# The values' products in 64x64 tiles of TensorE instead of 64x32, with another order of the operations

## The chip, the core and the metric

The kernel runs on one core of a Trainium2 chip. The metric is device time in microseconds (us) of one execution. Times of single instructions come from the trace of one profiled execution.

The engines are named as in the profile: PE is TensorE's matmul, PEld its weight load, DVE is VectorE, ACT is ScalarE, POOL is GpSimd, SP is SyncE, which here does nothing but issue DMAs. PSUM is the memory that PE writes.

## What is computed

Sliding-window attention with four sink positions, and behind it a gated layer whose gate is a causal convolution over five positions. Batch 4, 8 heads, 768 positions, 64 numbers per head, all in float32:

```python
scores = q @ k.transpose(0, 1, 3, 2) / sqrt(64)
keep   = (key < 4) | ((0 <= row - key) & (row - key < 128))
a      = softmax(where(keep, scores, -1e9))
x      = (a @ v), heads side by side -> (4, 768, 512)
gate   = sigmoid(sum over k of conv_w[k] * x shifted by 4 - k positions)
out    = (gate * (x @ w_val)) @ w_out
```

`w_val`, `w_out` and `conv_w` come as float64 and are decoded on the chip into a high and a low float32 part.

## The kernel before

The work is cut into 24 **steps**. Step s is one of 4 batches, one of 3 stretches of 256 positions (p = 0, 1, 2) and one of 2 groups of four heads; steps 2m and 2m+1 make **pair** m, for which the gated layer is computed. p is 0 for eight steps (0, 1, 6, 7, 12, 13, 18, 19) and over 0 for sixteen.

What a step does, with the names that the order uses:

- `kq`, `vv`: load k and q, or v, by SP (L236, L238, L245); three buffers each.
- `s0`, `s1` (`scores`, L391): 16 products each of 64x32 tiles of PE into one of two PSUM pairs `pr`; then DVE masks them (L396) and finds the maximum (L400 or L405).
- `e0`, `e1` (`exps`, L416) on ACT, `rec` the reciprocal of the sums, `norm` (L431) on POOL.
- `tx` (`probs_t`, L449): eight transposes on PE into a `pr` pair; `px` (DVE, L477 and L479) and `py` (ACT, L486) copy them to `wt`. `sk` transposes the sinks (L454).
- `vl` (`values`, L506): probabilities times v into the PSUM tile `xv`, of which there is one. For each of six blocks of keys (four where p = 0) there are four products (two heads by two groups), each cut in two halves of 32 output rows: 48 products a step, 32 where p = 0. Blocks have 64, 128, 192, 192, 128 and 64 moving columns (192, 192, 128, 64 where p = 0). Each float32 product runs as two loads and two matmuls, so that the trace has 96 (or 64) of each.
- `si` (`sinks`, L514) adds the sinks' share. `xc`, `xh`, `hd` (ACT, L521, L529, L533) copy x out, `c4` (POOL, L542) and `c0`, `c1` (DVE, L550) do the convolution out of `xv`. The values of step s+1 can start only when the convolution of step s has read `xv`.

For a pair, `v0` to `v3` (L569) multiply x by w_val, `g`, `h`, `l` gate (L588, L594, L598), `o0` to `o3` (L609) multiply by w_out and `t0`, `t1` (L613, L616) copy and store. `fill.n` is n matmuls on zeros. `scalars` (L100) reads the two numbers n_sink and window by two DMAs, each of which spreads 8 bytes to every partition; `flag` uses them at the very end.

Nothing is scheduled by the compiler: `ORDER` is a list of such names, written out, and each name's instructions go to the queues of their engines in that order. A load that stands behind another in the list stands behind it in SP's queue.

The inner lines of `values`:

```python
for e in range(2):
    r0 = o * D + e * QB                      # QB = 32, D = 64
    nc.tensor.matmul(acc[r0:r0 + QB, g, ...], v[js, g, n, e * QB:(e + 1) * QB],
                     t[js, g, n, a0:a1 + 1]...)
```

Of the kernel before, what the change touches and what calls it, by code (L numbers as in the profile page):

```python
# [36 lines left out]
wvl.0 masks fill.5 load_conv signs leads kq.0 conv_weights wva.0 blanks wvb.0 wvc.0 wvd.0 wvl.1 wva.1 s0.0
e0.0 s1.0 wvl.2 wva.2 fill.7 e1.0 wve.0 wvb.1 wvc.1 wvb.2 rec.0 kq.1 wvf.0 wvc.2 wvd.1 wol.0 woa.0 s1.1 e1.1
norm.0 s0.1 kq.2 e0.1 vv.0 fill.10 s1.2 e1.2 wve.1 wob.0 woc.0 tx.0 px.0 rec.1 fill.6 vv.1 py.0 sk.0 ts.0 sv.0
wvl.3 wod.0 wva.3 s0.2 e0.2 vl.0 kq.3 s0.3 wvf.1 si.0 xc.0 xh.0 norm.1 woe.0 c4.0 wvb.3 vv.2 wvd.2 wvc.3 tx.1  # L40
fill.6 px.1 wve.2 hd.0 rec.2 norm.2 wof.0 wvd.3 wve.3 e0.3 wol.1 kq.9 c0.0 c1.0 kq.4 tx.2 woa.1 wob.1 wvf.2
py.1 wol.3 sv.1 xl.0 sk.1 py.2 ts.1 wod.1 px.2 woc.1 vl.1 s1.3 si.1 wvf.3 sk.2 xc.1 ts.2 hd.1 c4.1 s0.4 xh.1
c0.1 e1.3 fill.4 rec.3 c1.1 e0.4 woe.1 woa.3 wob.3 xl.1 th.0 v0.0 v1.0 y0.0 g0.0 wol.2 woa.2 wod.3 wob.2
norm.3 s1.4 h0.0 th.1 l0.0 vl.2 si.2 xc.2 e1.4 v2.0 v3.0 woe.3 y1.0 woe.2 g1.0 tx.3 px.3 kq.6 s0.6 wof.1 o2.0
wod.2 wof.2 hd.2 c4.2 h1.0 xh.2 vv.4 py.3 rec.4 vv.3 l1.0 o0.0 c0.2 kq.5 s0.5 c1.2 e0.6 s1.6 wof.3 o1.0 t0.0
o3.0 e0.5 sk.3 ts.3 vv.6 th.2 norm.4 t1.0 vl.3 si.3 xh.3 xc.3 hd.3 sk.4 ts.4 xl.2 s1.5 xl.3 e1.5 c4.3 tx.4
v0.1 v1.1 px.4 rec.5 c0.3 vv.5 e1.6 c1.3 rec.6 v2.1 v3.1 kq.7 py.4 y0.1 g0.1 h0.1 s0.7 th.3 vl.4 norm.5 y1.1
g1.1 h1.1 s1.7 l0.1 kq.8 s1.8 l1.1 si.4 xc.4 c4.4 xh.4 o2.1 vv.8 o3.1 sv.6 hd.4 c0.4 tx.5 px.5 e0.7 e1.8 c1.4
o0.1 o1.1 t1.1 xl.4 e1.7 py.5 norm.6 tx.6 py.6 px.6 sk.5 ts.5 kq.15 rec.7 t0.1 vl.5 si.5 xc.5 c4.5 hd.5 xh.5
xl.5 vv.7 sk.6 ts.6 s0.9 norm.7 e0.9 s0.8 e0.8 c0.5 th.4 c1.5 rec.8 norm.8 v0.2 v1.2 tx.7 kq.10 py.7 v2.2 px.7  # L50
th.5 g0.2 s1.9 s1.10 h0.2 e1.9 vl.6 l0.2 si.6 xc.6 c4.6 hd.6 xh.6 sk.7 v3.2 ts.7 g1.2 h1.2 rec.9 l1.2 o2.2
e1.10 o0.2 o3.2 c0.6 c1.6 xl.6 sv.7 kq.11 tx.8 px.8 norm.9 s0.10 t1.2 py.8 vl.7 si.7 xc.7 hd.7 sk.8 ts.8 tx.9
kq.12 c4.7 xh.7 px.9 py.9 c0.7 xl.7 c1.7 e0.10 rec.10 o1.2 t0.2 v0.3 v1.3 th.6 s0.12 g0.3 th.7 s0.11 vv.10
e0.12 vl.8 s1.11 vv.13 si.8 h0.3 xc.8 c4.8 hd.8 xh.8 sk.9 ts.9 l0.3 e0.11 c0.8 v2.3 c1.8 norm.10 e1.11 v3.3
kq.13 g1.3 h1.3 o2.3 vv.9 s1.12 rec.11 s1.13 l1.3 vl.9 e1.12 vv.11 si.9 xc.9 hd.9 c4.9 tx.10 py.10 xh.9 o3.3
o0.3 o1.3 norm.11 px.10 rec.12 sv.13 tx.11 t1.3 c0.9 c1.9 sk.10 ts.10 s0.13 t0.3 py.11 px.11 kq.18 xl.9 th.8
vl.10 si.10 xl.8 v0.4 v1.4 xc.10 kq.14 c4.10 hd.10 xh.10 c0.10 c1.10 e1.13 e0.13 norm.12 v2.4 rec.13 g0.4
tx.12 s0.18 vl.11 sk.11 h0.4 v3.4 ts.11 si.11 py.12 px.12 norm.13 th.9 g1.4 h1.4 s1.14 s0.14 vv.12 xc.11 l0.4
l1.4 c4.11 hd.11 xh.11 sk.12 e0.14 ts.12 o0.4 o1.4 xl.11 c0.11 e1.14 c1.11 rec.14 o2.4 o3.4 sv.12 s0.15 xl.10
t0.4 vl.12 si.12 kq.16 xc.12 hd.12 xh.12 c4.12 tx.13 px.13 vv.22 t1.4 c0.12 th.11 c1.12 v2.5 e0.15 v3.5 g1.5  # L60
th.10 v0.5 v1.5 h1.5 g0.5 py.13 h0.5 sk.13 ts.13 norm.14 s1.15 e1.15 s1.18 vl.13 si.13 rec.15 kq.20 kq.17
e1.18 l0.5 l1.5 o0.5 s0.16 tx.14 px.14 o2.5 o3.5 xc.13 c4.13 vv.14 o1.5 hd.13 xh.13 e0.16 t1.5 norm.15 tx.15
c0.13 c1.13 sk.14 ts.14 th.12 py.14 px.15 vv.15 t0.5 s1.16 e0.18 xl.13 vl.14 si.14 xl.12 xc.14 c4.14 py.15
hd.14 xh.14 sk.15 th.13 ts.15 kq.19 v0.6 c0.14 c1.14 e1.16 v1.6 g0.6 rec.16 v2.6 vv.16 s0.17 rec.18 e0.17
s0.19 xl.14 vl.15 v3.6 g1.6 si.15 s1.19 vv.17 s1.17 norm.16 sk.16 ts.16 h0.6 l0.6 o0.6 h1.6 warm_up xc.15
hd.15 th.14 xh.15 e1.17 l1.6 c4.15 tx.16 o1.6 px.16 c0.15 c1.15 e0.19 rec.17 xl.15 v0.7 v1.7 g0.7 s0.20 py.16
# [5 lines left out]
rec.21 sk.19 ts.19 s1.22 s0.22 vl.19 h1.8 si.19 l1.8 sk.20 ts.20 h0.8 xc.19 l0.8 o0.8 kq.23 o1.8 c4.19 hd.19
xh.19 norm.21 vv.20 e1.22 o2.8 c0.19 c1.19 e0.22 rec.22 tx.21 py.21 xl.19 t0.8 px.21 s1.23 vl.20 s0.23 e1.23
si.20 norm.22 xc.20 c4.20 v0.9 v1.9 o3.8 th.18 hd.20 g0.9 xh.20 xl.20 e0.23 t1.8 tx.22 c0.20 v2.9 v3.9 rec.23
py.22 c1.20 h0.9 sk.21 norm.23 px.22 ts.21 th.19 g1.9 vl.21 si.21 tx.23 px.23 l0.9 o0.9 xc.21 h1.9 c4.21 l1.9
hd.21 xh.21 c0.21 o2.9 o3.9 t1.9 o1.9 c1.21 sk.22 vl.22 t0.9 ts.22 si.22 xc.22 py.23 xh.22 sk.23 xl.21 v0.10
# [773 lines left out]
```

## Time and profile before

| | us |
|---|---|
| time, median of 3 runs | 273.45 (273.35 to 273.96) |
| the profiled execution's own time | 275.11 |
| its span, first to last instruction | 273.3 |
| mean granted TensorE clock | 0.992 of 2.4 GHz |
| PE busy | 258.1 (94%) |
| DVE, ACT, POOL busy | 205.5, 188.3, 175.6 |

The profiled execution took 275.11 us, of which 273.3 are the span. Busy shares say how long an engine had something in work; several small matmuls lie over one another on PE, so that its busy time is no measure of how full the array is. What an operation costs on PE is read from the start of its first matmul to the start of the operation behind it.

### The profile page before, as it was taken

To read this page: it belongs to the slowest core of one execution; us is meant where nothing else is said; L and a number is where in the kernel's file an instruction comes from. 1 tells how busy PE (TensorE), PEld (TensorE's weight loads), DVE (VectorE), ACT (ScalarE), POOL (GpSimd) and SP (SyncE) were. 2 spreads that over 40 slices of the span, in tenths; PEclk is the share of its full clock that TensorE was granted. 3 is DMA by queue.
4 is the path that set the end of the run, shared out by engine and by line. 5 is a ranking of instruction groups with operands and counts; after the bars stand their busy time and mean duration, and the time that the engine had idled before them with its cause. 6 is when DMAs were issued, how large, how long until landed. Compare 5 with 4: busy or idle time off the path is not lost.

```text
span 273.3 us, 11512 instructions
## 1 busy us (share of the span) xinstructions
PE 258.1 (94%) x4779; PEld 218.1 (80%) x4784; DVE 205.5 (75%) x561; ACT 188.3 (69%) x667; POOL 175.6 (64%) x233
## 2 busy tenths in 40 slices
PE   7889999999999999999999999899799999999990
PEld 2456569789888899889889888799689899898970
DVE  5886999968879788978878788688577878724530
ACT  2899999788887859856567875687467667353410
POOL 6187886776758781797855575784883867734330
PEclk9999999999999999999999999999999999999996
DMA  6998355047274346448025764204336311040202
GB/s 202 389 377 294 135 155 166 2 142 256 60 208 133 104 140 177 141 135 260 4 55 185 240 180 138 60 4 133 126 93 228 115 41 42 4 137 2 77 5 82
DMA packets 27402, 37.07 MB, mean 136 GB/s; under 512 B 2256, under 2 KB 23760, under 8 KB 27344
## 3 DMA queue, kind: packets, MB, share of 16 engines
q1 hardware_dynamic: 26528, 35.48, 40.4%
q8 instruction: 39, 0.64, 1.0%
q10 hardware_dynamic: 816, 0.79, 0.9%
q14 instruction: 19, 0.16, 0.2%
HBM read 29.97 MB, written 6.29 MB: 133 GB/s over the span
## 4 chain that ended last, share of the span: by engine, by line
PE 82%; ACT 8%; DVE 3%; DMA 2%; issue 2%; POOL 1%; ACTq 0%
PE ac L609 25%; PE ac L569 24%; PE xv L506 11%; PE pr L391 10%; PE pr L449 7%; PE xv L514 3%; ACT w L416 3%; DMA raw<-in_w_val_dram 2%; DVE sg L550 1%; PE ac L454 1%; ACT wv_p L137 1%; ACT wv_p L156 1%; POOL xl L537 0%; DVE wt L477 0%; ACT xt L521 0%
## 5 line engine op out<-in xcount | busy, mean ns | idle before, releaser
L550 DVE SCALAR_TENSOR_TENSOR sg<-xv,cw,sg 128x256 f32<-128x256 f32 x192 | 77.4, 473 | 10.1 <-POOL sg L542 8.7
L431 POOL TENSOR_TENSOR wx<-w,sm 128x512 f32<-128x512 f32 x48 | 49.1, 1046 | 7.7 <-DVE sm L423 7.6
L416 ACT ACTIVATE w<-pr,ngm 128x132 f32<-128x132 f32 x136 | 48.5, 369 | 1.8
L569 PE MATMUL ac<-xh,wvh 128*128 128x256 f32 x192 | 48.3, 286 | 0.0
L598 POOL TENSOR_TENSOR gl<-sg,gh 128x512 fp32r<-128x512 f32 x24 | 31.0, 1295 | 26.8 <-ACT gh L594 26.7
L569 PE MATMUL ac<-xh,wvl 128*128 128x256 f32 x192 | 47.2, 280 | 0.0
L542 POOL TENSOR_TENSOR sg<-xt,cw 128x512 f32<-128x512 f32 x24 | 25.0, 1043 | 28.4 <-ACT xt L521 26.0
L391 PE MATMUL pr<-k,q 64*32 64x168 f32 x1536 | 36.5, 307 | 4.1 <-DVE ngm L400 1.4
L609 PE MATMUL ac<-woh,gh 128*128 128x512 f32 x96 | 39.2, 408 | 0.0
L506 PE MATMUL xv<-wt,v 64*32 64x192 f32 (+2 forms) x2048 | 37.0, 275 | 1.8 <-issue 1.3
L506 PEld LDWEIGHTS xv<-wt,v 64*32 64x32 f32 x2048 | 34.8, 105 | 4.2 <-issue 2.3
L609 PE MATMUL ac<-wol,gh 128*128 128x512 f32 x96 | 38.0, 395 | 0.0
L609 PE MATMUL ac<-woh,gl 128*128 128x512 f32 x96 | 37.9, 395 | 0.0
L569 PEld LDWEIGHTS ac<-xh,wvh 128*128 128x128 f32 x192 | 36.1, 188 | 0.5 <-issue 0.3
L569 PEld LDWEIGHTS ac<-xh,wvl 128*128 128x128 f32 x192 | 36.2, 189 | 0.2
L391 PEld LDWEIGHTS pr<-k,q 64*32 64x32 f32 x1536 | 24.1, 106 | 11.9 <-ACT w L416 3.2
L537 POOL TENSOR_TENSOR xl<-xt,xh 128x512 fp32r<-128x512 f32 x24 | 30.9, 1289 | 3.6 <-ACT xt L521 1.7
L569 PE MATMUL ac<-xl,wvh 128*128 128x256 f32 x192 | 30.6, 280 | 0.3 <-POOL xl L537 0.3
L594 ACT ACTIVATE gh<-sg 128x512 fp32r<-128x512 f32 x24 | 15.2, 632 | 19.9 <-DVE sg L588 19.8
L396 DVE COPY_PREDICATED pr<-low,pr 128x256 f32<-128x256 uint8 x48 | 20.3, 422 | 9.9 <-PE pr L391 8.8
L416 ACT ACTIVATION_READ_ACCUMULATOR w<-pr,ngm 128x1 f32 x136 | 27.6, 203 | 0.0
L521 ACT ACTIVATE xt<-xv 128x512 f32<-128x512 f32 x24 | 14.4, 598 | 18.9 <-PE xv L514 18.7
...
## 6 DMA issues: line engine op xcount, KB each, us to landing
...
out_dram<-osb SPq DMA_DIRECT2D x24, 256.0 KB, 2.2
q<-in_qt_dram SPq DMA_DIRECT2D x23, 256.0 KB, 5.0
...
v<-in_vt_dram SPq DMA_DIRECT2D x8, 256.0 KB, 3.8
...
```

What stands on the lines that cost most here:

```text
L391: nc.tensor.matmul(ss[e * QB:(e + 1) * QB, j, c * n + x0:c * n + x1], q[js, g, (4 * c + e) * QB:(4 * c + e + 1) * QB], k[js, g, (2 * c + e ...
L396: nc.vector.copy_predicated(sv[:, :, :, :D], low[:, None, None, :].to_broadcast([P, 2, 2, D]), sv[:, :, :, 2 * HB:])
L416: nc.scalar.activation(out=w[:, g, j, c], in_=sx[:, j, c, :PK], func=AF.Exp, scale=0.125 if whole else -1.0, bias=ngm[:, g, j, c:c + 1], a ...
L431: nc.gpsimd.tensor_tensor(out=t[:, n].rearrange("p c h x -> p h c x"), in0=w[:, :, :, at], in1=sm.to_broadcast([P, 4, 2, D]), op=ALU.mult)
L449: nc.tensor.transpose(out=x[:, n, o:o + P], identity=ident, in_=ws[s][:, n, c, 2 * g:2 * g + 2].rearrange("p j x -> p (j x)"))
L506: nc.tensor.matmul(acc[r0:r0 + QB, g, x0 + h * D:x0 + (h + a1 - a0 + 1) * D], v[js, g, n, e * QB:(e + 1) * QB], t[js, g, n, a0:a1 + 1].rea ...
L537: nc.gpsimd.tensor_tensor(out=half(xls, s, "xl", F32R), in0=xts[s], in1=half(xhs, s, "xh", F32R).bitcast(F32), op=ALU.subtract)
L542: nc.gpsimd.tensor_tensor(out=half(sg, s, "sg", F32), in0=xts[s], op=ALU.mult, in1=cw[:, g, KT - 1:].to_broadcast([P, 2, PQ]))
L550: nc.vector.scalar_tensor_tensor(out=g, in0=x, scalar=a, in1=g, op0=ALU.mult, op1=ALU.add)
L569: nc.tensor.matmul(acc[:, h], a[:, kc, cs], x[:, kc], start=(n == 0), stop=(n == 11))
L598: nc.gpsimd.tensor_tensor(out=gl, in0=g, in1=gh.bitcast(F32), op=ALU.subtract)
L609: nc.tensor.matmul(acc, a[:, kc, ts], x[:, kc], start=(kc + n == 0), stop=(kc + n == 5))
```

## The change

`values` no longer cuts a product in two: one product has 64 output rows, a 64x64 tile of PE. There are four tiles in the array where there were eight, each with the same moving columns as before; a step has 24 products (16 where p = 0) instead of 48 (32).

```diff
             for g, j, o in tiles:
                 js = slice(j * D, (j + 1) * D)
                 h = n - 2 + a0
-                for e in range(2):
-                    r0 = o * D + e * QB
-                    nc.tensor.matmul(acc[r0:r0 + QB, g, x0 + h * D:x0 + (h + a1 - a0 + 1) * D],
-                                     v[js, g, n, e * QB:(e + 1) * QB],
-                                     t[js, g, n, a0:a1 + 1].rearrange("p a r -> p (a r)"),
-                                     start=(n == n0), stop=False, skip_group_check=True)
+                nc.tensor.matmul(acc[o * D:(o + 1) * D, g, x0 + h * D:x0 + (h + a1 - a0 + 1) * D], v[js, g, n],
+                                 t[js, g, n, a0:a1 + 1].rearrange("p a r -> p (a r)"),
+                                 start=(n == n0), stop=False, skip_group_check=True)
```

`ORDER` is another list of the same names. Two lines of it, of the stretch around step 16 to 18:

```diff
-vl.16 si.16 norm.18 sk.18 ts.18 e1.19 vv.18 norm.17 t0.6 xc.16 c4.16 hd.16 xh.16 e0.20 tx.18 px.18 scalars
-py.18 th.15 v2.7 v3.7 c0.16 g1.7 h1.7 l1.7 tx.17 c1.16 kq.21 xl.16 py.17 rec.19 px.17 sv.18 o2.6 o3.6 t1.6
...
+ts.17 l0.7 o0.7 si.17 e1.20 xc.17 hd.17 xh.17 norm.19 tx.19 c4.17 vv.19 c0.17 sv.18 c1.17 xl.17 o1.7 kq.22
+o2.7 o3.7 py.19 e0.21 rec.20 norm.20 px.19 t1.7 s1.21 scalars vl.18 t0.7 si.18 xc.18 hd.18 xh.18 c4.18 c0.18
```

Most of PE's row of operations stays as it was; neighbours change places. On PE, values stand directly behind scores 18 times before and 14 times now, and scores directly behind values 5 times before and 7 times now. The 38 matmuls on zeros are kept.

The first place is SP's queue around `scalars`. In the kernel before the two reads of n_sink and window stand ahead of the load of k and q for step 21 (the L236 and L238 rows behind them):

```order
L616 DMA out_dram<-osb 128x512
L100 DMA nw_raw<-in_n_sink_dram 128x2
L100 DMA nw_raw<-in_window_dram 128x2
L236 DMA k<-in_kt_dram 128x2x408
L238 DMA q<-in_qt_dram 128x2x256
L616 DMA out_dram<-osb 128x512
```

In the changed kernel (lines behind `values` have moved up by three) the first L236 and L238 here load step 21, and the reads come behind a load for step 22:

```order
L236 DMA k<-in_kt_dram 128x2x408
L238 DMA q<-in_qt_dram 128x2x256
L245 DMA v<-in_vt_dram 128x2x384
L245 DMA v<-in_vt_dram 128x2x256
L249 DMA vs<-in_vsk_dram 128x256
L613 DMA out_dram<-osb 128x512
L245 DMA v<-in_vt_dram 128x2x256
L249 DMA vs<-in_vsk_dram 128x256
L236 DMA k<-in_kt_dram 128x2x408
L238 DMA q<-in_qt_dram 128x2x256
L613 DMA out_dram<-osb 128x512
L100 DMA nw_raw<-in_n_sink_dram 128x2
```

So the two reads have moved behind two stores and two loads of k and q: from ahead of step 21's load to behind step 22's.

The second place is PE's row at the values of step 20. Before (transposes of step 21, scores s1.23, the values, scores s0.23):

```order
L449 MATMUL pr_87<-ident,wx 128x128 x8
L391 MATMUL pr_86<-k,q 32x168 x16
L506 MATMUL xv<-wt,v 32x64 x8
L506 MATMUL xv<-wt,v 32x128 x8
L506 MATMUL xv<-wt,v 32x192 x16
L506 MATMUL xv<-wt,v 32x128 x8
L506 MATMUL xv<-wt,v 32x64 x8
L391 MATMUL pr_87<-k,q 32x168 x16
L514 MATMUL xv<-skt,vh 128x256 x2
```

And now:

```order
L449 MATMUL pr_87<-ident,wx 128x128 x8
L504 MATMUL xv<-wt,v 64x64 x4
L504 MATMUL xv<-wt,v 64x128 x4
L504 MATMUL xv<-wt,v 64x192 x8
L504 MATMUL xv<-wt,v 64x128 x4
L504 MATMUL xv<-wt,v 64x64 x4
L391 MATMUL pr_86<-k,q 32x168 x16
L391 MATMUL pr_87<-k,q 32x168 x16
L511 MATMUL xv<-skt,vh 128x256 x2
```

The values come ahead of a call of scores that stood ahead of them, so that one operation less lies between them and the sinks of step 19. The same is done for steps 7 (scores) and 10 (transposes), and at step 12 one call of scores has left the stretch.

## Rows read from the trace of the kernel before

**Rows 1.** The page: busy time, clock by 40 slices, chain by engine and line.
```profile
PE 258.1 (94%) x4779; PEld 218.1 (80%) x4784; DVE 205.5 (75%) x561; ACT 188.3 (69%) x667; POOL 175.6 (64%) x233
...
PEclk9999999999999999999999999999999999999996
...
PE 82%; ACT 8%; DVE 3%; DMA 2%; issue 2%; POOL 1%; ACTq 0%
PE ac L609 25%; PE ac L569 24%; PE xv L506 11%; PE pr L391 10%; PE pr L449 7%; PE xv L514 3%; ACT w L416 3%; DMA raw<-in_w_val_dram 2%; DVE sg L550 1%; PE ac L454 1%; ACT wv_p L137 1%; ACT wv_p L156 1%; POOL xl L537 0%; DVE wt L477 0%; ACT xt L521 0%
```

**Rows 2.** Stretch 40 to 260 us: each engine's busy time and count, clock, DMA.
```profile
40.00:260.00 220.00, 216.91 (x4234) 193.20 (x4233) 170.54 (x458) 152.97 (x545) 145.29 (x180) 1.00 0.38 119
```

**Rows 3.** What PE waited for: total us, times, longest.
```profile
PE pr L391 <- DVE ngm L400: 1.4, 1, 1.4
PE xv L506 <- issue: 1.3, 1, 1.3
```

**Rows 4.** PE's groups by shape: count, busy us, mean ns of one.
```profile
L506 PE MATMUL xv<-wt,v 64*32 64x192 f32 x768 | 22.5, 324 | 0.4 <-ACT wt L486 0.2
L506 PE MATMUL xv<-wt,v 64*32 64x128 f32 x640 | 20.8, 272 | 0.1
L506 PE MATMUL xv<-wt,v 64*32 64x64 f32 x640 | 15.4, 219 | 1.3 <-issue 1.3
```

**Rows 5.** PE in order of time: start, length, operation; values behind scores, p over 0.
```profile
121.66 0.80 PE L391 MATMUL pr<-k,q 64*32 64x168 f32 x32
122.26 1.68 PE L506 MATMUL xv<-wt,v 64*32 64x64 f32 x96
123.86 0.51 PE L514 MATMUL xv<-skt,vh 128*128 128x256 f32 x2
```

**Rows 6.** PE: values behind a transpose, p over 0.
```profile
77.73 1.59 PE L506 MATMUL xv<-wt,v 64*32 64x64 f32 x96
79.25 0.51 PE L514 MATMUL xv<-skt,vh 128*128 128x256 f32 x2
```

**Rows 7.** PE: values behind scores, p = 0.
```profile
150.67 1.25 PE L506 MATMUL xv<-wt,v 64*32 64x192 f32 x64
151.85 0.50 PE L514 MATMUL xv<-skt,vh 128*128 128x256 f32 x2
```

**Rows 8.** PE: scores ahead of transposes.
```profile
153.67 0.80 PE L391 MATMUL pr<-k,q 64*32 64x168 f32 x32
154.41 0.55 PE L449 MATMUL pr<-ident,wx 128*128 128x128 f32 x3
```

**Rows 9.** PE around scores s1.20, s0.21; in brackets the idle time before.
```profile
191.80 0.80 PE L391 MATMUL pr<-k,q 64*32 64x168 f32 x32
194.02 0.81 PE L391 MATMUL pr<-k,q 64*32 64x168 f32 x32 [1.42 <-DVE ngm L400]
```

**Rows 10.** SP's queue, 186 to 188 us; DVE's last copy for step 17.
```profile
186.46 0.42 SPq L100 DMA_DIRECT2D nw_raw<-in_n_sink_dram  x1
186.92 0.46 SPq L100 DMA_DIRECT2D nw_raw<-in_window_dram  x1
187.42 0.43 SPq L236 DMA_DIRECT2D k<-in_kt_dram  x1
187.90 0.47 SPq L238 DMA_DIRECT2D q<-in_qt_dram  x1
...
191.37 0.68 DVE L479 TENSOR_TENSOR wt<-pr,prev 128x512 f32<-128x512 f32 x1
```

**Rows 11.** DMA issues of 184 to 196 us: KB, us from issue to landing.
```profile
q<-in_qt_dram SPq DMA_DIRECT2D x1, 256.0 KB, 5.9
```

**Rows 12.** PE around the values of step 15.
```profile
168.73 1.59 PE L506 MATMUL xv<-wt,v 64*32 64x64 f32 x87
171.59 0.32 PE L506 MATMUL xv<-wt,v 64*32 64x64 f32 x9 [1.27 <-issue]
```

**Rows 13.** Step 19's convolution on DVE, then PE's row up to values of step 20.
```profile
216.63 3.23 DVE L550 SCALAR_TENSOR_TENSOR sg<-xv,cw,sg 128x256 f32<-128x256 f32 x8 [0.98 <-POOL sg L542]
...
218.98 1.03 PE L449 MATMUL pr<-ident,wx 128*128 128x128 f32 x8
219.95 0.80 PE L391 MATMUL pr<-k,q 64*32 64x168 f32 x32
220.54 1.66 PE L506 MATMUL xv<-wt,v 64*32 64x64 f32 x95
```

**Rows 14.** Step 22's convolution on DVE and the values of step 23 on PE.
```profile
245.56 3.22 DVE L550 SCALAR_TENSOR_TENSOR sg<-xv,cw,sg 128x256 f32<-128x256 f32 x8
...
248.97 1.59 PE L506 MATMUL xv<-wt,v 64*32 64x64 f32 x96
```

**Rows 15.** PE's weight loads by shape: count, busy us, mean ns of one.
```profile
L506 PEld LDWEIGHTS xv<-wt,v 64*32 64x32 f32 x2048 | 34.8, 105 | 4.2 <-issue 2.3 <-PE ac L609 0.6 <-ACT wt L486 0.6
L449 PEld LDWEIGHTS pr<-ident,wx 128*128 128x128 f32 x192 | 21.7, 141 | 3.0 <-POOL wx L431 1.0 <-issue 0.5
```

More of the change, by code (lines that the diff above doesn't have):

```diff
@@ L36 @@
 ORDER = """
[L37 to L66, printed above, removed]
@@ L67 @@
-vl.16 si.16 norm.18 sk.18 ts.18 e1.19 vv.18 norm.17 t0.6 xc.16 c4.16 hd.16 xh.16 e0.20 tx.18 px.18 scalars
-py.18 th.15 v2.7 v3.7 c0.16 g1.7 h1.7 l1.7 tx.17 c1.16 kq.21 xl.16 py.17 rec.19 px.17 sv.18 o2.6 o3.6 t1.6
-s1.20 s0.21 h0.7 vl.17 l0.7 sk.17 e1.20 ts.17 rec.20 o0.7 vv.19 norm.19 si.17 xc.17 c4.17 hd.17 xh.17 xl.17
-tx.19 px.19 c0.17 o2.7 e0.21 o1.7 py.19 o3.7 th.16 c1.17 t0.7 s1.21 kq.22 vl.18 si.18 norm.20 sv.19 xc.18
-c4.18 th.17 hd.18 xh.18 t1.7 xl.18 tx.20 px.20 py.20 c0.18 vv.21 v2.8 c1.18 e1.21 v3.8 g1.8 v0.8 v1.8 g0.8
@@ L72 @@
[L72 to L76, printed above, removed]
@@ L77 @@
-v1.10 c4.22 th.20 ts.23 hd.22 g0.10 c0.22 th.21 c1.22 v2.10 v3.10 h0.10 xl.22 l0.10 o2.10 g1.10 h1.10 vv.23
-vl.23 si.23 o0.10 xc.23 l1.10 o1.10 hd.23 xh.23 t0.10 xl.23 o3.10 t1.10 v0.11 c4.23 c0.23 v1.11 th.22 c1.23
-th.23 v2.11 g0.11 h0.11 v3.11 g1.11 h1.11 l0.11 l1.11 o2.11 o0.11 o1.11 t0.11 o3.11 t1.11 flag
+blanks wvl.0 load_conv kq.0 masks signs leads fill.5 wvl.1 conv_weights wvl.2 wva.0 wvb.0 s0.0 kq.1 wvd.0
+wvc.0 s1.0 wve.0 fill.4 wva.1 wvb.1 e0.0 wva.2 e1.0 wvb.2 wvc.2 fill.7 wvd.1 wol.0 kq.2 s1.1 wvc.1 rec.0 wvl.3
@@ new lines @@
+s0.1 fill.10 s1.2 wvf.0 woa.0 e1.1 wve.1 e0.1 wob.0 norm.0 tx.0 px.0 e1.2 woc.0 rec.1 py.0 vv.0 fill.6 sv.0
+sk.0 ts.0 wod.0 wva.3 norm.1 s0.2 e0.2 vl.0 kq.8 kq.3 s0.3 wvf.1 si.0 xc.0 woe.0 wvb.3 xh.0 tx.1 c4.0 rec.2
+wof.0 wol.2 wol.1 wvc.3 fill.6 hd.0 wvd.2 wve.2 px.1 wvd.3 kq.4 wve.3 e0.3 c0.0 c1.0 woa.1 wob.1 wvf.2 norm.2
+vv.3 py.1 vv.1 sv.1 xl.0 tx.2 py.2 sk.1 px.2 woc.1 ts.1 vl.1 s1.3 wvf.3 wod.1 si.1 xc.1 c4.1 sk.2 ts.2 s0.4
+hd.1 xh.1 xl.1 c0.1 woe.1 e1.3 wol.3 rec.3 woa.3 c1.1 wob.3 e0.4 v0.0 v1.0 th.0 y0.0 norm.3 vv.2 g0.0 vl.2
@@ new lines @@
+woa.2 wob.2 h0.0 l0.0 th.1 s1.4 kq.6 kq.5 wof.1 woe.3 e1.4 v2.0 v3.0 y1.0 tx.3 py.3 si.2 xc.2 woe.2 hd.2 xh.2
+g1.0 px.3 wof.2 wod.2 s0.6 c4.2 c0.2 h1.0 o0.0 l1.0 o2.0 e0.6 wof.3 s0.5 c1.2 rec.4 xl.2 s1.6 wod.3 o1.0 o3.0
+t0.0 norm.4 sk.3 e0.5 ts.3 t1.0 vl.3 si.3 xh.3 xc.3 xl.3 s1.5 e1.6 tx.4 px.4 vv.5 sk.4 ts.4 hd.3 c4.3 c0.3
+e1.5 rec.5 norm.5 v0.1 v1.1 y0.1 py.4 c1.3 th.2 v2.1 v3.1 g0.1 h0.1 kq.7 s0.7 vv.4 th.3 vl.4 y1.1 g1.1 vv.6
+l0.1 s1.7 rec.6 sv.6 s1.8 h1.1 si.4 xh.4 l1.1 xc.4 hd.4 e0.7 o2.1 o3.1 c4.4 c0.4 xl.4 e1.8 kq.10 kq.9 c1.4
@@ new lines @@
+norm.6 tx.5 o0.1 t1.1 py.5 o1.1 px.5 sk.5 e1.7 tx.6 rec.7 px.6 ts.5 t0.1 py.6 vl.5 si.5 xc.5 hd.5 xh.5 s0.9
+e0.9 sk.6 ts.6 s0.8 e0.8 c4.5 c0.5 c1.5 xl.5 vv.7 v0.2 rec.8 v1.2 norm.7 tx.7 py.7 px.7 th.4 g0.2 v2.2 s1.9
+s1.10 norm.8 th.5 h0.2 e1.9 vl.6 si.6 sk.7 vv.8 v3.2 ts.7 xc.6 hd.6 xh.6 l0.2 g1.2 rec.9 o0.2 c4.6 h1.2 l1.2
+o2.2 o3.2 sv.7 e1.10 c0.6 kq.11 tx.8 c1.6 py.8 vl.7 px.8 norm.9 s0.10 si.7 t1.2 sk.8 xl.6 xc.7 hd.7 xh.7 ts.8
+kq.12 c4.7 tx.9 px.9 c0.7 c1.7 e0.10 rec.10 py.9 xl.7 th.6 o1.2 norm.10 v0.3 v1.3 vv.10 g0.3 h0.3 s0.12 s0.11
@@ new lines @@
+t0.2 vl.8 si.8 s1.11 e0.12 xc.8 hd.8 c4.8 sk.9 ts.9 l0.3 kq.13 th.7 vv.9 xh.8 e0.11 e1.11 c0.8 c1.8 v2.3 v3.3
+o2.3 xl.8 g1.3 s1.12 s1.13 vl.9 si.9 h1.3 tx.10 l1.3 o3.3 e1.12 rec.12 rec.11 px.10 xc.9 hd.9 xh.9 py.10 c4.9
+c0.9 t1.3 o0.3 o1.3 c1.9 th.9 t0.3 sk.10 ts.10 xl.9 vv.11 norm.11 s0.13 vl.10 si.10 xc.10 c4.10 hd.10 xh.10
+norm.12 kq.15 tx.11 px.11 py.11 th.8 e0.13 v0.4 v1.4 v2.4 v3.4 c0.10 c1.10 g0.4 sk.11 ts.11 e1.13 g1.4 h0.4
+l0.4 kq.14 tx.12 py.12 vl.11 px.12 s0.14 s1.14 rec.13 si.11 h1.4 sk.12 ts.12 o0.4 l1.4 o1.4 vv.12 o2.4 o3.4
@@ new lines @@
+sv.12 xc.11 c4.11 hd.11 xh.11 c0.11 vv.13 c1.11 e0.14 sv.13 kq.18 s0.18 norm.13 e1.14 rec.14 kq.16 s0.15 xl.10
+t1.4 vl.12 si.12 th.11 xc.12 hd.12 xh.12 xl.11 c4.12 t0.4 xl.12 tx.13 norm.14 px.13 v2.5 v3.5 c0.12 g1.5 py.13
+th.10 c1.12 e0.15 v0.5 v1.5 g0.5 sk.13 ts.13 h0.5 l0.5 vv.14 s1.15 e1.15 s1.18 rec.15 kq.19 vl.13 si.13 xc.13
+hd.13 xh.13 o0.5 s0.16 h1.5 kq.17 tx.14 px.14 c4.13 c0.13 c1.13 l1.5 o2.5 o3.5 th.12 e0.16 o1.5 norm.15 t1.5
+py.14 warm_up tx.15 py.15 t0.5 sk.14 ts.14 s1.16 vl.14 si.14 vv.17 e1.18 xc.14 hd.14 xh.14 sk.15 ts.15 xl.13
@@ new lines @@
+px.15 e1.16 c4.14 vv.15 v2.6 v0.6 v1.6 c0.14 c1.14 rec.16 g0.6 s0.17 xl.14 e0.18 h0.6 e0.17 s0.19 rec.18 vl.15
+norm.16 v3.6 l0.6 th.13 si.15 vv.16 g1.6 s1.19 xc.15 th.14 c4.15 hd.15 xh.15 s1.17 sk.16 o0.6 ts.16 kq.20 h1.6
+l1.6 xl.15 tx.16 o1.6 v0.7 v1.7 e0.19 px.16 c0.15 e1.17 rec.17 t0.6 kq.21 c1.15 s0.20 py.16 vl.16 si.16
+norm.18 vv.21 sk.18 ts.18 vv.18 e1.19 xc.16 hd.16 g0.7 norm.17 rec.19 e0.20 tx.18 px.18 py.18 c4.16 c0.16
+th.15 xh.16 v2.7 v3.7 xl.16 h0.7 g1.7 tx.17 h1.7 px.17 l1.7 c1.16 py.17 o2.6 o3.6 s1.20 s0.21 t1.6 vl.17 sk.17
@@ new lines @@
+ts.17 l0.7 o0.7 si.17 e1.20 xc.17 hd.17 xh.17 norm.19 tx.19 c4.17 vv.19 c0.17 sv.18 c1.17 xl.17 o1.7 kq.22
+o2.7 o3.7 py.19 e0.21 rec.20 norm.20 px.19 t1.7 s1.21 scalars vl.18 t0.7 si.18 xc.18 hd.18 xh.18 c4.18 c0.18
+sv.19 th.17 tx.20 px.20 e1.21 vv.22 rec.21 th.16 v2.8 v3.8 v0.8 v1.8 g1.8 h1.8 c1.18 g0.8 sk.19 ts.19 py.20
+h0.8 s1.22 kq.23 s0.22 vl.19 si.19 xc.19 hd.19 xh.19 xl.18 l1.8 sk.20 l0.8 vv.20 o0.8 ts.20 c4.19 c0.19 c1.19
+norm.21 e1.22 e0.22 rec.22 o1.8 o2.8 tx.21 py.21 px.21 t0.8 vl.20 xl.19 s1.23 s0.23 si.20 xc.20 norm.22 hd.20
@@ new lines @@
+xh.20 e1.23 th.18 v0.9 v1.9 g0.9 c4.20 c0.20 e0.23 rec.23 o3.8 t1.8 tx.22 v2.9 v3.9 h0.9 py.22 c1.20 sk.21
+l0.9 norm.23 th.20 ts.21 th.19 vl.21 si.21 g1.9 px.22 xc.21 hd.21 xh.21 tx.23 px.23 o0.9 o2.9 c4.21 c0.21
+c1.21 h1.9 l1.9 xl.20 o3.9 t1.9 o1.9 py.23 sk.22 ts.22 t0.9 vl.22 xl.21 si.22 xc.22 sk.23 v0.10 v1.10 xh.22
+ts.23 v2.10 v3.10 g0.10 c4.22 hd.22 c0.22 c1.22 th.21 g1.10 h0.10 l0.10 o2.10 vv.23 vl.23 h1.10 si.23 xc.23
+hd.23 xh.23 l1.10 xl.22 o0.10 o1.10 c4.23 c0.23 xl.23 t0.10 c1.23 o3.10 v0.11 th.22 v1.11 t1.10 v2.11 v3.11
@@ L80 @@
+g0.11 th.23 g1.11 h0.11 l0.11 o2.11 h1.11 l1.11 o0.11 o1.11 flag t0.11 o3.11 t1.11
 """
```

## The prediction

> **What bounds the kernel now.** First the page: PE is busy for 94% of the span, no other engine for more than 75%, and the chain that ended last is PE for 82% [rows 1]. The reader should see in it that the chain runs through all of PE's lines in turn, the values (L506) with 11%. Then the stretch from 40 to 260 us alone: PE is busy for 216.91 of 220 us, at a granted clock of 1.00 [rows 2]. There is no gap to fill there: a shorter operation on PE shortens the end, and a wait of PE lengthens it by its whole length. Then PE's waits: two are above a microsecond in that stretch, 1.4 us in scores, put down to DVE, and 1.3 us in values, with "issue" as the releaser [rows 3]. So the change counts by three things: what the values cost on PE, what becomes of the two waits, and which new waits the order makes.
>
> **The values on PE.** Half as many products sounds like half the time, and the rows say no. One matmul takes 219, 272 and 324 ns for 64, 128 and 192 columns [rows 4]: 52.5 ns for each further 64 columns, on a fixed part that overlaps with the neighbours. A step with p over 0 has 64, 128, 192, 192, 128 and 64 columns, 12 pieces of 64, each run twice: 24 x 52.5 = 1.26 us for one tile of the array. Where p = 0 there are 9 pieces, 0.95 us. All tiles run side by side, so this is the array's time whether there are eight narrow ones or four wide ones. From the start of the values to the start of what follows the trace has 1.52 us behind a transpose [rows 6], 1.60 behind scores [rows 5], and 1.18 for p = 0 [rows 7]. Most of it is the 1.26 or 0.95 that stays.
>
> The rest is two things. One is the change of shape, from 64x32 tiles to the full array. A call of scores takes 0.60 us to the start of values, which have its own shape [rows 5], but 0.74 to the start of transposes [rows 8]: 0.14 us for a change. Taken off 1.52 and 1.18, that leaves 0.12 and 0.09 us, about 0.10, in which eight tiles start and end one behind the other. With four tiles there are three such gaps, not seven: 0.06 us saved. No row has 64x64 tiles, so the bounds are 0 (the gaps are by columns loaded) and 0.10 (they vanish). I take 0.06, the count of gaps. A step then costs 1.46, or 1.12 us.
>
> Before, 11 steps with p over 0 stand behind scores, 5 don't, and 8 have p = 0: 11 x 1.60 + 5 x 1.52 + 8 x 1.18 = 34.6 us. After: 16 x 1.46 + 8 x 1.12 = 32.3. That is 2.3 us less, but scores and values now have different shapes. The 18 scores ahead of values cost 0.60 instead of 0.74, and this is lost: 18 x 0.14 = 2.5 us. In 5 places scores followed values without a change; I take half of 0.14 each, 0.35 us, between none and all. Sum: **+0.55 us**, bounds -0.4 (gaps vanish) and +2.0 (gaps stay).
>
> That a change between two shapes of 64 rows costs what one to 128 rows costs is assumed; no row shows one. Were it free, the 21 places where scores and values meet in the new order would give back 21 x 0.14 = 2.9 us.
>
> The Trainium skill ("TensorEngine Tiling (Array Packing)", Key Properties) says that a change of tiling mode, as against a change of tile, drains TensorE. By that rule the 64x32 tiles were the better choice next to scores, which speaks against this change; the trace agrees as far as it goes, with 0.14 us for 64x32 to 128 rows, and shows no change between two shapes of 64 rows.
>
> **The wait of 1.4 us in scores.** PE stops between s1.20 and s0.21 [rows 9]. The profile names DVE, but the copy that s0.21 needs had ended at 191.37 + 0.68 = 192.05, two microseconds earlier. What comes late is q of step 21: issued at 187.90, right behind the two reads of n_sink and window [rows 10], and landed 5.9 us later, at 193.8 [rows 11]; PE goes on at 194.02. In the new order this load stands ahead of those reads, by two stores and a further load of k and q, many microseconds before its use. The reads now stand ahead of a store, of v for step 22 and of k and q for step 23, which are used over 10 us later by the count of operations between. Next late would be the copy of 192.05, which s1.20 covers. I take the whole wait away: **-1.4 us** (between -1.4 and 0).
>
> **The stop of 1.3 us in values.** At step 15 PE stands still after 87 of 96 matmuls with nothing that the profile shows [rows 12]; no data can be missing so late in one operation, so I read it as a stream of instructions that came late. The same scores, scores, values follow one another in the new order, but the values bring half the instructions. That may avoid it, or it may happen elsewhere: half of it, **-0.65 us**, bounds -1.3 and 0.
>
> **The new order.** Values wait for the convolution of the step before to leave the one `xv` tile. At step 19 that ends at 216.63 + 3.23 = 219.86, and values follow behind transposes and one call of scores [rows 13]. The new order puts values ahead of that call, at 219.95 by PE's row. The tightest start behind a convolution is 248.97 - 245.56 - 3.22 = 0.19 us after it [rows 14], so 220.05: a wait of 0.1 us. At steps 7, 10 and 12 one operation less stands there too, of 0.74 us (scores) or 0.83 (transposes start at 218.98, the next at 219.95, less 0.14 for the change of shape); the copies and reciprocals ahead of these convolutions are also earlier in DVE's and ACT's lists. Bounds: 0.1 and 3 x 0.74 + 0.83 = 3.1 us; I take **+0.2**, near the row that is there. The first 40 us and the end keep their row of operations but for neighbours: nothing.
>
> **Sum**: 0.55 - 1.4 - 0.65 + 0.2 = -1.3 us on the profiled execution's own 275.11, so 273.8. The runs' median of 273.45 is 0.6% lower; the same 1.3 us off it gives **272.1 us**.
>
> **The rivals.**
>
> *The order's gain is taken back at `xv`.* The four earlier values each wait for the convolution, by up to the operation that was moved behind them. For it: the convolution takes the same time, and its slack was already down to 0.2 us in places [rows 14]. Against it: DVE's lists are shifted for it. Between 272.1 and 272.1 + 2.9 = 275.0, in the middle 273.5. It decides from 1.3 us of waits upward: with more, the kernel is slower than before.
>
> *Weight loads come into the open.* A load takes 105 ns for 32 columns and 141 for 128 [rows 15], twice the 52.5 ns that a block of 64 columns streams. With eight tiles in flight loads hide: 96 of them fit into 1.52 us, 16 ns each. With four, a tile might stand still for 105 - 52.5 = 52.5 ns at each pass of a 64-column block: four passes a step, two where p = 0. 16 x 0.21 + 8 x 0.105 = 4.2 us: 276.3, slower. It decides from 1.3/24, 0.055 us, a step. Against it: the step's 1.52 us leave room for almost no exposed load today.
>
> *The change of shape among 64-row tiles is free.* The 2.9 us above: 269.2. For it: the row tiling is the same in both. Against it: every change that the trace has costs 0.14.
>
> **How the numbers follow.** The forecast, between 271.0 and 273.2: 0.47. Gain lost at `xv`: 0.33. Exposed loads: 0.11. Free change: 0.09. The range leaves out the last two: from 270.0 (forecast with the gaps gone and the whole stop avoided, 270.5, and a little of the free change) to 275.0. A measurement of this kernel can tell about 0.2%, 0.55 us, from no change. Faster: 0.39 of the forecast, 0.06 of the second case and 0.09 of the last, together 0.54. Same: 0.08 and 0.12, 0.20. Slower: 0.15 and 0.11, 0.26.
>
> **What would show it.** Values of 1.46 and 1.12 us from start to start; scores ahead of values 0.74, not 0.60; no wait over 1 us at s0.21, and q of step 21 landed long before. A values step over 1.6 us behind a transpose would speak for exposed loads, scores of 0.60 ahead of values for the free change, and waits of PE put down to DVE's L550 for `xv`. The forecast is wrong if a step of values comes out far from its 1.26 us of streaming, or if new waits add up to over a microsecond.

## The result, and the profile after

The changed kernel takes 270.36 us (median of 6 runs, 269.86 to 272.06), against 274.13 us (273.35 to 274.49) for the kernel before, in runs on the same chip: a ratio of 0.988, with an interval of 0.984 to 0.991. It is faster by 1.2%. The prediction was 272.1 us, in a range of 270.0 to 275.0; it forecast a gain of 1.3 us, and the measured one, 3.8 us, is nearly three times that. Medians here are of all runs of a kernel, ratios and intervals of its undisturbed runs alone, so that a median and its ratio need not match to the last digit.

The page of the changed kernel, as far as it answers to [rows 1], with the row of the DMA queue that carries instructions (blocks, MB, share). In the kernel before that row read 39, 0.64, 1.0%:

```profile
span 268.7 us, 9474 instructions
...
PE 258.3 (96%) x3760; PEld 213.6 (79%) x3760; DVE 205.4 (76%) x561; ACT 189.1 (70%) x667; POOL 176.2 (66%) x233
...
PEclk9999999999999999999999999999999999999996
...
q8 instruction: 31, 0.51, 0.8%
...
PE 83%; ACT 9%; POOL 2%; DMA 2%; issue 1%; DVE 0%; POOLq 0%; ACTq 0%
```

PE is still the bound, at the same clock, and its busy time is the 258 us of before. What shrank is the time in which it is not busy: 15.2 us before, 10.4 now. The longest of PE's waits (total us, times, longest):

```profile
PE pr L209 <- DVE warm L758: 1.2, 1, 1.2
PE ac L180 <- POOL wv_f L157: 0.6, 1, 0.6
PE pr L391 <- DMA q<-in_qt_dram: 0.6, 1, 0.6
```

All three are in the first 11 us. The two rows of [rows 3] are gone, the wait in scores and the stop in values, and none has taken their place; no row of the list has "issue" as its releaser any more.

The values themselves. PE in order of time, behind scores (p over 0), behind two calls of scores (p = 0), and step 20; start, length, operation:

```profile
119.26 0.80 PE L391 MATMUL pr<-k,q 64*32 64x168 f32 x32
119.99 1.55 PE L504 MATMUL xv<-wt,v 64*64 64x64 f32 x48
121.47 0.51 PE L511 MATMUL xv<-skt,vh 128*128 128x256 f32 x2
...
149.07 1.21 PE L504 MATMUL xv<-wt,v 64*64 64x192 f32 x32
150.21 0.50 PE L511 MATMUL xv<-skt,vh 128*128 128x256 f32 x2
...
214.44 1.04 PE L449 MATMUL pr<-ident,wx 128*128 128x128 f32 x8
215.42 1.55 PE L504 MATMUL xv<-wt,v 64*64 64x64 f32 x48
216.90 1.49 PE L391 MATMUL pr<-k,q 64*32 64x168 f32 x64
```

From start to start a step takes 121.47 - 119.99 = 1.48 us, or 1.14 where p = 0; before it took 1.60 or 1.52, and 1.18 [rows 5 to 7]. Scores ahead of values take 119.99 - 119.26 = 0.73 us, where they took 0.60 [rows 5]. So half the products make a step 0.04 to 0.12 us shorter, and the scores in front of it give back 0.13.

Where the time went, then, is read by stretches. The start of the values of steps 3 and 17 before (those of 15 and 23 are in [rows 12, 14]), with step 9 and the end of step 15:

```profile
56.94 1.59 PE L506 MATMUL xv<-wt,v 64*32 64x64 f32 x96
...
113.13 2.11 PE L506 MATMUL xv<-wt,v 64*32 64x64 f32 x96
115.17 0.51 PE L514 MATMUL xv<-skt,vh 128*128 128x256 f32 x2
...
171.84 0.38 PE L569 MATMUL ac<-xh,wvh 128*128 128x256 f32 x1
...
194.59 1.69 PE L506 MATMUL xv<-wt,v 64*32 64x64 f32 x96
```

And steps 3, 15, 17 and 23 after, with the scores s1.20 and s0.21 in one row ahead of step 17:

```profile
55.58 1.55 PE L504 MATMUL xv<-wt,v 64*64 64x64 f32 x48
...
165.93 1.37 PE L391 MATMUL pr<-k,q 64*32 64x168 f32 x64
167.23 1.55 PE L504 MATMUL xv<-wt,v 64*64 64x64 f32 x48
168.71 0.38 PE L566 MATMUL ac<-xh,wvh 128*128 128x256 f32 x1
...
188.69 1.37 PE L391 MATMUL pr<-k,q 64*32 64x168 f32 x64
190.00 1.55 PE L504 MATMUL xv<-wt,v 64*64 64x64 f32 x48
...
244.30 1.55 PE L504 MATMUL xv<-wt,v 64*64 64x64 f32 x48
```

| stretch | before, us | after, us | difference |
|---|---|---|---|
| to the values of step 3 | 56.94 | 55.58 | -1.36 |
| step 3 to step 15 | 111.79 | 111.65 | -0.14 |
| step 15 to step 17 | 25.86 | 22.77 | -3.09 |
| step 17 to step 23 | 54.38 | 54.30 | -0.08 |
| sum | | | -4.67 |

In the third stretch before, the values of step 15 take 171.84 - 168.73 = 3.11 us [rows 12] where 1.60 is usual, a stop of 1.51; and s1.20 with s0.21 takes 194.59 - 191.80 = 2.79 us [rows 9], while two calls without a wait between them take 193.04 - 191.88 = 1.16 us to the values (in the run with one load moved, below): a wait of 1.63. Together that is the -3.1. In the second stretch before, step 9 takes 115.17 - 113.13 = 2.04, a stop of 0.44 that the prediction had not seen. Without it the twelve steps of that stretch have become 0.30 us longer, not shorter. So all of the gain behind step 3 is time in which PE stood still, and none of it is PE's work. The two profiled executions differ by more than the medians do: 4.6 us by their spans, 3.77 us by the medians.

### The profile page after: what moved, and what is told of

It reads as the page before. It is cut to its first block, busy times and chain, and to the rows that moved or that the text cites. A ratio compares the mean times of both kernels' runs of the same rounds, so it can differ in the third digit from the quotient of the medians.

```text
span 268.7 us, 9474 instructions
## 1 busy us (share of the span) xinstructions
PE 258.3 (96%) x3760; PEld 213.6 (79%) x3760; DVE 205.4 (76%) x561; ACT 189.1 (70%) x667; POOL 176.2 (66%) x233
## 4 chain that ended last, share of the span: by engine, by line
PE 83%; ACT 9%; POOL 2%; DMA 2%; issue 1%; DVE 0%; POOLq 0%; ACTq 0%
PE ac L606 25%; PE ac L566 25%; PE xv L504 11%; PE pr L391 10%; PE pr L449 7%; ACT w L416 4%; PE xv L511 3%; DMA raw<-in_w_val_dram 2%; PE ac L454 1%; POOL xl L534 1%; ACT wvh L151 1%; ACT wv_p L137 1%; ACT wv_p L156 1%; ACT wvl L183 1%; POOL wo_f L157 0%
## 5 line engine op out<-in xcount | busy, mean ns | idle before, releaser
L391 PE MATMUL pr<-k,q 64*32 64x168 f32 x1536 | 35.3, 307 | 0.7 <-DMA q<-in_qt_dram 0.6
L504 PEld LDWEIGHTS xv<-wt,v 64*64 64x64 f32 x1024 | 30.4, 133 | 7.0 <-issue 4.5
L504 PE MATMUL xv<-wt,v 64*64 64x192 f32 (+2 forms) x1024 | 34.5, 278 | 0.2 <-PE ac L566 0.2
```

Of the source, the lines that this page charges most:

```text
L391: nc.tensor.matmul(ss[e * QB:(e + 1) * QB, j, c * n + x0:c * n + x1], q[js, g, (4 * c + e) * QB:(4 * c + e + 1) * QB], k[js, g, (2 * c + e ...
L504: nc.tensor.matmul(acc[o * D:(o + 1) * D, g, x0 + h * D:x0 + (h + a1 - a0 + 1) * D], v[js, g, n], t[js, g, n, a0:a1 + 1].rearrange("p a r ...
```

## The experiments

**Three runs on who earns the gain, tiles or order.** The first has the order of before with 64x64 tiles:

```diff
 ORDER: as in the kernel before
-for e in range(2): ... products of 32 output rows
+one product of 64 output rows
```

> Only the tiles are changed: values in 64x64 tiles, the order of the kernel before. If the time came from the order, as I think, this stands within 1.5 us of the kernel before: values at 1.48 and 1.14 us from start to start and scores ahead of them at 0.73 (net +0.2 to +0.9 us on PE), the wait of 1.4 us at s0.21 stays, and only the stop of 1.3 us inside the values of step 15 may be gone (273 to 274.5 us beside 274). If the wide tiles themselves gave the time, it is 271 us or less.

Measured: 272.0 us, a ratio of 0.989 (0.986 to 0.993). The wide tiles alone give 1.1%, against the first theory, and the time lies below the 273 to 274.5 us that went with it. The trace has steps of 1.48 and 1.14 us and no stop in values. It also settles what s0.21 waits for. PE in order of time:

```profile
189.70 0.80 PE L391 MATMUL pr<-k,q 64*32 64x168 f32 x32
190.85 0.81 PE L391 MATMUL pr<-k,q 64*32 64x168 f32 x32 [0.35 <-DMA q<-in_qt_dram]
```
Here the profile names q itself, not DVE. It was issued at 184.79, landed 5.8 us later at 190.59, and PE went on at 190.85.

The second run has the new order with 64x32 tiles:

```diff
 ORDER: as in the changed kernel
-one product of 64 output rows
+for e in range(2): ... products of 32 output rows
```

> Only the order is changed: the new order, values in 64x32 tiles as before. If the order gave the time, the wait at s0.21 is gone (-1.4 us) and this stands 1.5 to 3.5 us below the kernel before, 270.5 to 272.5 us; the 14 scores ahead of values take 0.60 us again. A stop without a releaser inside a values call would show that the instruction stream of 64x32 values is what makes it. If the wide tiles gave the time, this is at 274 us.

Measured: 278.37 us (274.95 to 280.14), a ratio of 1.009 (1.005 to 1.013). The order alone makes the kernel slower, by 0.9%, and neither theory had that. Its longest waits, PE around the two largest, and the granted clock by 40 slices:

```profile
PE pr L391 <- issue: 3.1, 2, 2.4
PE xv L506 <- issue: 1.8, 1, 1.8
```
```profile
132.52 1.06 PE L391 MATMUL pr<-k,q 64*32 64x168 f32 x37
135.98 0.79 PE L391 MATMUL pr<-k,q 64*32 64x168 f32 x27 [2.40 <-issue]
...
173.00 1.59 PE L506 MATMUL xv<-wt,v 64*32 64x64 f32 x87
176.39 0.32 PE L506 MATMUL xv<-wt,v 64*32 64x64 f32 x9 [1.79 <-issue]
...
PEclk9999999999999999999989999999999999999998
```

The stop of step 15 is there too, after the same 87 of 96 matmuls, and larger; another of 2.40 us stands in the middle of scores. The new order does not avoid stops: they are longer in it, as long as the values bring 96 matmuls.

Part of the loss is the clock. PE stood still for 2.40 us, worked for 1.45 us, and from 137.43 to 140.84 us the granted clock was 0.50, the lower of its two levels (1.2 GHz). Matmuls of 512 columns followed one another every 0.43 us there, and every 0.23 us behind it; half of the 3.41 us, some 1.7 us, is the estimated price. Two of the twelve runs took 274.95 and 275.24 us, no longer than the kernel before, at a mean clock of 0.995 and 0.994; the other ten took 277.8 to 280.1 us at 0.983 to 0.990.

The third run is the kernel before with one load moved:

```diff
-... px.18 scalars py.18 ... c1.16 kq.21 xl.16 ...
+... px.18 kq.21 scalars py.18 ... c1.16 xl.16 ...
```

> The kernel before with one thing moved: the load of k and q for step 21 stands ahead of the two reads of n_sink and window instead of behind them. If q of step 21 is what s0.21 waits for, the wait of 1.42 us ahead of s0.21 is gone, the load lands in about 4 us, and the kernel is 1.4 us faster (-0.5%). If DVE is what it waits for, as the profile names it, nothing changes.

Measured: 272.95 us, a ratio of 0.993 (0.990 to 0.996). The expected 0.5% is in the interval, though q landed 5.2 us after its issue (186.74), not about 4. In the trace s1.20 and s0.21 are one row, with the values right behind:

```profile
191.88 1.37 PE L391 MATMUL pr<-k,q 64*32 64x168 f32 x64
193.04 1.28 PE L506 MATMUL xv<-wt,v 64*32 64x64 f32 x60
```

So the late q of step 21 was the wait, and its place behind the reads of n_sink and window the reason. The stops stayed: 1.9 us by the list of waits, at step 9 and step 15.

**The kernel before once more.**

> The kernel before again, unchanged, for a second profile. If the stop of 1.3 us inside the values of step 15 belongs to the program, it is there again at the same matmul; if it is chance, it is absent or elsewhere. The first part of w_val, on which ACT starts at 6.69 us in one profile of before and at 5.80 us in that of the changed kernel, shows by how much this start varies without any change; I expect between 5.8 and 6.7 us.

Measured: 276.11 us, one execution. The stop of step 15 and the wait at s0.21 are where they were, with the same 9 matmuls left and the same wrong name:

```profile
172.77 0.32 PE L506 MATMUL xv<-wt,v 64*32 64x64 f32 x9 [1.34 <-issue]
...
195.15 0.81 PE L391 MATMUL pr<-k,q 64*32 64x168 f32 x32 [1.35 <-DVE ngm L400]
```

The stop of step 15 therefore belongs to the program and not to chance. That of step 9 does not come in every execution: 0.44 us in the first profile, none in this one, where the step takes 1.52 us. The trace's DMA records have a block of instructions landing shortly before PE goes on, behind every long stop seen: at 170.06 before 171.59 in the kernel before, at 171.42 before 172.77 here, at 134.76 before 135.98 and 175.11 before 176.39 in the second run. That is 1.2 to 1.5 us each time. The theory from here on: PE runs out of instructions, and what counts is how many of them a stretch brings.

**As many products with wide tiles, pieces in a row.** The changed kernel with each product cut in pieces of 64 columns, the pieces of one product behind one another:

```diff
-matmul(acc[..., x0 + h*D : x0 + (h + a1 - a0 + 1)*D], v[js, g, n], t[js, g, n, a0:a1 + 1])
+for x in range(a0, a1 + 1):
+    matmul(acc[..., x0 + (h + x - a0)*D : ... + D], v[js, g, n], t[js, g, n, x])
```

> The changed kernel (64x64 tiles, new order) with every product of the values issued in pieces of 64 columns: the same tiles and the same columns streamed, but 48 products a step again (36 where p = 0), so as many instructions on PE as with 64x32 tiles. Theory: what the narrow tiles cost is the supply of PE's instructions, which falls behind where small products follow one another, and PE then stands still until 1.2 to 1.5 us after the next 16 KB block of its instructions has landed. Then stops without a releaser of 1 us and more come back, two or more, about 39 blocks are fetched instead of 31, and the time is 273 to 278 us. Rival: the narrow tiles themselves are slow (their starts and ends one behind the other, the shape of the weight loads); then there are no such stops and the time stays within 1 us of the changed kernel, at about 270 to 272 us.

Measured: 292.05 us, a ratio of 1.065 (1.062 to 1.068), and neither theory said that. There is no stop in the trace. The steps themselves are long:

```profile
80.12 2.45 PE L505 MATMUL xv<-wt,v 64*64 64x64 f32 x96
82.50 0.50 PE L511 MATMUL xv<-skt,vh 128*128 128x256 f32 x2
```

2.38 us instead of 1.48, 2.04 instead of 1.14 where p = 0: 24 x 0.9 = 21.6 us, all of the loss. The run can't tell the theories apart, because PE got through its instructions so much more slowly. The likely reason is that neighbours in PE's row now lie in the same tile, while the other three tiles stand idle. The Trainium skill ("TensorE: Matmul & The Clock Gate", Part 3, The mechanism) says that matmuls start and end in the order of the program, while loads for other rows may be drawn ahead; the trace agrees, since the same matmuls in another order of the program take 1.56 us (next run) instead of 2.38.

**As many products with wide tiles, tiles in the inner loop.** The same pieces with the loops exchanged, so that neighbours lie in different tiles again:

```diff
 for n in range(n0, 6):
-    for g, j, o in tiles:
-        matmul(..., t[js, g, n, a0:a1 + 1])
+    for x in range(a0, a1 + 1):
+        for g, j, o in tiles:
+            matmul(..., t[js, g, n, x])
```

> The changed kernel with each product of the values cut in pieces of 64 columns, the pieces in the outer loop and the four tiles in the inner one: 48 products a step as in the kernel before, but four 64x64 tiles, and neighbouring products in the instruction stream lie in different tiles (in the run with the pieces of one product one behind the other, a step took 2.385 us instead of 1.478 and the kernel 292 us). If that loss came from neighbours in the same tile, a step takes 1.5 to 1.7 us here (1.26 us of streaming and the gaps). Theory (PE's instructions come late when there are too many of them in a short time): instruction reads are back at about 39 or 40 blocks, one or more stops of 1 us or over put down to issue are back, and the kernel takes 273 to 277 us. Rival (the stops belong to 32-row tiles or to the order): no stop, 271 to 272 us, or, if a step takes 1.7 us, up to 275 with every us of it in the steps.

Measured: 274.86 us, a ratio of 1.003 (1.0005 to 1.006): the whole gain is gone. PE at step 10, and at the two stops, and the row of the instruction queue:

```profile
122.42 1.63 PE L505 MATMUL xv<-wt,v 64*64 64x64 f32 x96
123.98 0.50 PE L511 MATMUL xv<-skt,vh 128*128 128x256 f32 x2
...
23.35 0.77 PE L391 MATMUL pr<-k,q 64*32 64x168 f32 x23
25.30 0.49 PE L391 MATMUL pr<-k,q 64*32 64x168 f32 x9 [1.19 <-issue]
...
218.59 1.89 PE L505 MATMUL xv<-wt,v 64*64 64x64 f32 x96
220.42 1.04 PE L391 MATMUL pr<-k,q 64*32 64x168 f32 x34
222.43 0.80 PE L391 MATMUL pr<-k,q 64*32 64x168 f32 x30 [0.97 <-issue]
```
```profile
q8 instruction: 40, 0.66, 1.0%
```

This is the run that tells the theories apart. Tiles, order, shape changes and loads of data are those of the changed kernel; the pieces are narrower, and PE's matmuls and weight loads are as many as before (9696, against 9563). A step takes 1.56 us (1.21 where p = 0), 0.08 (0.07) more than in the changed kernel: 16 x 0.08 + 8 x 0.07 = 1.8 us. The stops are back, 2.2 us in two places, and neither at step 15. With 0.27 us at step 20, where the values take 220.42 - 218.59 = 1.83 us, that is 4.3 of the 4.7 us by which the spans differ. The stops come with the number of instructions, not with the width of a tile and not with the order. The number alone is not enough: with the same 9696 in 290 us the run above had none. The last block landed at 23.94 and 220.96, 1.4 and 1.5 us before PE went on.

**Old order, q first, wide tiles.** The first and the third run together:

> The order of the kernel before with the load for step 21 ahead of the two reads, and 64x64 tiles: two parts of the change and nothing else of the new order. If these two are what the change is worth, it stands with the changed kernel, 1.2% under the kernel before (270.5 to 271.5 us). If the rest of the new order is worth something, the changed kernel is faster than this one by more than 0.5 us.

Measured: 271.77 us, a ratio of 0.991 (0.988 to 0.995), no better than the wide tiles alone. The profiled execution (273.61 us) lost elsewhere what it had won at s0.21, in values that waited 1.5 us for v (at 113 us). That wait is in no other profile; loads that arrive close to their use in the old order may explain it, which was not tested.

**Wide tiles in two steps only.** The kernel before with 64x64 tiles at the two steps that had stops, 9 and 15:

```diff
-for e in range(2):
+qb = D if s in (9, 15) else QB
+for e in range(D // qb):
```

> The kernel before with 64x64 tiles in the values of steps 9 and 15 alone, the two calls in which PE stood still for 0.3 and 1.4 us. If a stop is made by the instructions of that stretch, both are gone, and the kernel is 1 to 1.7 us faster than before; the wait of 1.5 us at s0.21 stays. If the stop depends on the whole stream up to there, one turns up in another call of values or scores, and the time stays with before.

Measured: 273.96 us, a ratio of 0.998 (0.9955 to 1.0002), not told from the kernel before. Both stops are gone, and others have come or grown, all away from those steps:

```profile
PE ac L178 <- issue: 1.4, 1, 1.4
...
PE pr L391 <- issue: 1.2, 1, 1.2
PE ac L610 <- ACT sm L422: 0.9, 1, 0.9
...
PE xv L515 <- issue: 0.6, 1, 0.6
```

The row with L422 is one of them under a wrong name: PE goes on at 195.97, 1.33 us behind the landing of a block (194.64), while L422 had ended at 195.24. The stop at L178 is there in the kernel before as well, with 0.2 us. Together that is some 4 us: a stop that is driven out of one place comes back in another as long as the program has this many instructions. The instruction queue still has 39 blocks here. The wait at s0.21, expected to stay, is down to 0.7 us.

**The changed kernel once more**, beside the last two:

> The changed kernel again, unchanged, beside the others: 270 to 271.5 us, 31 blocks of PE instructions, no stop above 0.5 us behind 40 us. A stop here would say that the fetches also fall behind with the wide tiles, by chance.

Measured: 271.37 us, a ratio of 0.991 (0.988 to 0.994); no stop, 31 blocks, span 268.6. Beside 271.77 for the old order with q first, the new order is worth 0.15% by the medians, which these runs can't tell from zero. Beside the wide tiles alone (0.989) it is not told from zero either.

## Why the prediction was right, point by point

**What bounds the kernel.** Right. No gain came from PE's work, and all of it from PE's waits.

**The values on PE.** Right in step and scores. The streaming that stays was read from the slope of 52.5 ns per 64 columns; after the change it is the same within 3 ns. The rows by shape:

```profile
L504 PE MATMUL xv<-wt,v 64*64 64x192 f32 x384 | 20.4, 327 | 0.0
...
L504 PE MATMUL xv<-wt,v 64*64 64x64 f32 x320 | 12.6, 227 | 0.2 <-PE ac L566 0.2
```

(327 - 227) / 2 = 50 ns. The steps were forecast at 1.46 and 1.12 us and measured at 1.48 and 1.14; the scores ahead of them at 0.74 and 0.73. By the stretch from step 3 to 15, twelve steps cost 0.30 us more, so 24 cost some 0.6 more, where +0.55 and +0.2 for the order's waits were forecast together: 0.15 us too much. By what the stops, the wait and the start leave of the 4.67 us it is +0.27, half a microsecond too much.

**The change of shape.** The assumption that no row showed, that a change between 64x32 and 64x64 costs what one to 128 rows costs, was right: 0.13 us by these rows. That rules out the free change, 269.2 us. The Trainium skill's rule that a change of tiling mode drains the engine ("TensorEngine Tiling (Array Packing)", Key Properties) says so too; the trace agrees with a price of 0.13 us, and shows nothing of how it comes about.

**Weight loads in the open.** Ruled out by the 1.48 us. A load of 64 columns takes 133 ns, longer than the 50 ns of a block, and stays hidden:

```profile
L504 PEld LDWEIGHTS xv<-wt,v 64*64 64x64 f32 x1024 | 30.4, 133 | 7.0 <-issue 4.5 <-PE ac L606 0.6 <-ACT wt L486 0.6
```

**The wait at s0.21.** Right in cause and nearly in size: -1.4 forecast, -1.63 measured. SP's issue of q for step 21 after the change stands 11 us ahead of its use:

```profile
177.96 0.50 SPq L238 DMA_DIRECT2D q<-in_qt_dram  x1
```

Reading the trace against the name that the profile gave (DVE, already done two microseconds before) was what made this step work. But the order was not the only way to it: with wide tiles alone the same wait shrank to 0.35 us, since q was issued 4.9 us ahead of s1.20 there (184.79 to 189.70) and 3.9 before (187.90 to 191.80).

**The stop in values.** The mechanism was right and the size was not. It was counted at -0.65 us, half of the one stop of 1.3. Measured: 1.51 us at step 15 and 0.44 at step 9, both gone, -1.95. Two things were missed. The bracket in the trace understates a stop (1.27 against 1.51 by the starts of operations), and the shorter stop at step 9 does not stand in the list of waits at all, only in a step of 2.04 us. And "half" was no estimate: with a fifth of PE's instructions gone (7520 instead of 9563) the stops vanish in all four profiles with 64x64 tiles and whole products, and with the count restored, tiles in the inner loop, they come back. Of the 1.95 us, the 0.44 at step 9 is in part luck of the execution: the second profile of the kernel before does not have it.

**The start.** Forecast at nothing, measured at -1.36 us up to step 3. Of this, 0.87 us is there at the first scores, ahead of any values (7.11 us before, 6.24 after). The runs with one load moved and with wide tiles in two steps have the same ramp up to there as the kernel before, and their first scores start at 6.38 and 6.43: most of the 0.87 us is a difference from execution to execution. ACT begins with w_val when its first read lands: its first copy starts at 6.69 us before and 5.80 after. In the other profiles with 64x32 tiles it starts at 5.85 to 6.72, in those with 64x64 tiles and whole products at 5.42 to 5.80, so a part may also be one of the kernels. Small stops in the ramp (0.2 to 1.4 us at L178 around 25 us, in the four profiles of the old order with narrow tiles there) belong to it as well. How the rest of the 1.36 us divides stays open.

**The new order.** Forecast at +0.2, four places where values might wait for `xv`. There is no such wait: at step 20 the transposes take 215.42 - 214.44 = 0.98 us to the start of the values, the 0.97 that they take before scores [rows 13]. The rival in which the gain was taken back at `xv` falls with it. What the forecast missed about the order is that alone it would have been slower.

In the sum: -1.3 forecast and -4.67 by the starts of the values of step 23. The stops account for 1.3 of the 3.4 us between, the start for 1.4, the wait for 0.2, values and order for 0.5. The direction and the range were right, by a sum of which one term was too small and one was missing.

**Where luck helped.** The forecast's own case was 271.0 to 273.2 us, and 270.36 lies below it. The range reached down to 270.0 for gaps that vanish and a change of shape that is partly free, and neither came; the second stop and the start, which the prediction did not have, brought the time there. The credit also went to the wrong half of the change: by its terms the order earns 1.4 - 0.2 = 1.2 us and the tiles 0.65 - 0.55 = 0.1 us. Alone, the tiles take 1.1% off and the order adds 0.9%. The halves do not add up, because each changes what the other meets: with the tiles alone the wait at s0.21 shrinks too, and with the order alone the stops grow.
